# Folding row sums: a small TensorE product, or GpSimd copies a pair ahead and a VectorE addition

## The chip, the cores and the metric

The kernel runs on one core of one Trainium2 chip. The metric is the device time of one execution in microseconds (us). Differences under 1% are read with the 95% interval of several rounds, taken on the same chip as runs of the kernel before. A profile is one execution; the four runs of the kernel before differ by up to 4 us, and the profiled one (1109.11 us) is 1.5 us below their median.

## The reference

Attention with normalised queries and keys (8 batches, 12 heads, 448 positions, head size 64), then a feed-forward block with w_in, softmax-times-input, a layer norm and w_out. The part that the change touches is the first line of the attention:

```python
def rmsnorm(x, g):
    rms = np.sqrt(np.mean(x * x, axis=-1, keepdims=True) + 1e-06)
    return x / rms * g
q_n, k_n = (rmsnorm(q, g_q), rmsnorm(k, g_k))
...
h = x @ w_in            # x: 3584 x 768, w_in: 768 x 1024
...
return (ln @ w_out)     # w_out: 1024 x 768
```

## The kernel before

The kernel goes through 48 pairs of heads. A pair's q and k lie in SBUF with each row of 64 elements split in two halves of 32, on partitions that are 32 apart. So a sum of squares comes out as two partial sums, `part` (128x28), and the two halves have to be added across partitions. A constant matrix and a small product did that:

```python
fold = consts.tile([P, 2, 2, 32], FP32, name="fold")
...
ps_t = ctx.enter_context(tc.tile_pool(name="ps_t", bufs=6, space=bass.MemoryType.PSUM))
...
def row_sums(n):
    d["part"] = small.tile([P, 2 * NB], FP32, tag="part", name="part")
    nc.vector.tensor_reduce(d["part"], d["sq"], AX, OP.add)

def fold_sums(n):
    d["ss"] = ps_t.tile([P, 2 * NB], FP32, tag="t", name="ss")
    nc.tensor.matmul(d["ss"], fold.rearrange("p h x t -> p (h x t)"), d["part"], start=True, stop=True)

def rsqrt_seed(n):
    nc.scalar.activation(d["y"], d["ss"], AF.Ln, scale=1.0 / D, bias=eps)
    nc.vector.tensor_scalar(d["x"], d["ss"], -0.5 / D, -0.5e-6, OP.mult, OP.add)
    nc.scalar.activation(d["y"], d["y"], AF.Exp, scale=-0.5)
# then rsqrt_step (VectorE) and normalise: qkn = qk * y (GpSimd)
```

The `ss` tile is one of six PSUM banks that also serve the scores `s`, the values product `o`, the exponentials' sums `sm`, the transposed activations `pu` and the results `po`. Two other parts matter for the argument: work that GpSimd and VectorE share, and the copies that empty `pu`.

```python
def add(n, kc):                       # sum of the exponentials over four chunks
    if kc == 1:
        nc.gpsimd.tensor_tensor(d["es"], d["E"][:, 0], d["E"][:, 1], OP.add)
    else:
        nc.vector.tensor_tensor(d["es"], d["es"], d["E"][:, kc], OP.add)

def fields():                         # first step of a weight's conversion, VectorE
    nc.vector.tensor_scalar(tmp[:, 1], hi, 0xFFFFF, None, OP.bitwise_and)
    nc.vector.tensor_scalar(e, hi, 20, 0x7FF, OP.logical_shift_right, OP.bitwise_and)
def product():                        # its last step, for w_in on GpSimd
    nc.gpsimd.tensor_tensor(dst[:, c, cols], m, e.bitcast(FP32), OP.mult)

def ff_transpose(t):
    for half in range(2):
        pt = ps_t.tile([P, 4, P], FP32, tag="t", name="pu")
        ...                           # four transposes on TensorE
        (nc.vector.tensor_copy if half else nc.scalar.copy)(d["uT"][:, 4 * half : 4 * half + 4], pt)
```

The main loop issues, per pair n (each `unit` is followed by whatever `later` put off to that unit):

```python
for n in range(N):
    ...
    unit(lambda: scores(n, 0)); qk_transpose(n + 1)
    unit(lambda: scores(n, 1)); fold_sums(n + 2)      # later: seed, step, normalise of n + 2
    ff(0)                                             # feed-forward work of earlier tokens
    unit(lambda: values(n - 1)); row_sums(n + 3)
    unit(lambda: sums(n - 1)); ff(1)
    unit(lambda: scores(n, 2)); unit(lambda: scores(n, 3)); ff(2)
```

## Time and profile before

| | before |
|---|---|
| time, median of 4 runs (range) | 1110.59 us (1107.99 to 1111.8) |
| span of the profiled execution | 1107.3 us |
| the product: passes, busy | 96, 20.7 us |
| to about 160 us | w_in is converted, VectorE bounds, 11.11 us a pair |
| to about 335 us | w_out is converted, mostly VectorE |
| from about 335 to 950 us | TensorE never idle |

The utilisation rows, the stages and one period are shown with the prediction below. Two groups of instructions (line, engine, operation, output and inputs, shapes, count | busy us, mean ns of one | idle time before them, and what ended it). L467 is the `fields` step of w_in, L529 the product:

```profile
L467 DVE TENSOR_SCALAR tmp<-raw 128x512 uint32<-128x512 uint32 x12 | 14.6, 1216 | 0.0
L529 PE MATMUL ss<-part,fold 128*128 128x28 f32 x96 | 20.7, 298 | 13.5 <-DVE part L524 12.1 <-ACT E L576 0.8 <-DVE r L617 0.6
```

The passage from the VectorE stage to the TensorE stage (start, length, engine, line, operation):

```profile
339.51 0.41 PE L529 MATMUL ss<-part,fold 128*128 128x28 f32 x2
339.76 1.07 PE L676 MATMUL pu<-ident,u 128*128 128x128 f32 x8
340.76 3.23 PE L595 MATMUL o<-E,v 112*64 112x448 f32 x16
344.67 5.42 PE L635 MATMUL h<-w_in,xT 128*128 128x512 f32 x12
```

### The profile page before, as it was taken

Reading aid. Unit: us, or ns where it says so; the run is one execution under the profiler, and the core shown is the slowest. Engines: PE = TensorE matmul, PEld = TensorE weight load, DVE = VectorE, ACT = ScalarE, POOL = GpSimd, SP = SyncE. Lnnn points to the kernel's source line nnn. Section 1 sums busy time; section 2 is a strip of 40 time slices with the busy share of each in tenths; the row PEclk is TensorE's granted clock in tenths of the full one; section 3 lists DMA queues with packets and bytes.
Section 4 is the critical chain, followed back from the end, with each engine's and each line's share of the span. In section 5 each row is a group of like instructions: output and inputs, shape, how many; then the busy total and the mean of one; then the engine's idle time right before and its main releaser. Section 6 shows DMA issues by size and latency. Waiting matters only on the chain.

```text
span 1107.3 us, 10659 instructions
## 1 busy us (share of the span) xinstructions
PE 1035.3 (93%) x3617; PEld 475.6 (43%) x3617; DVE 605.4 (55%) x1018; ACT 370.6 (33%) x773; POOL 240.3 (22%) x155
## 2 busy tenths in 40 slices
PE   3988888888789999999999999999999999999997
PEld 1323233333234444444444444444444444455554
DVE  3999996569997444444444444454446644522300
ACT  3656553235564222222222222332224322311110
POOL 2565651123223111111111011121112211100000
PEclk9899999998989999999999999999999999999999
DMA  7454544014543111111111111121111100000010
GB/s 140 89 122 98 124 87 85 23 39 93 112 88 62 40 40 40 39 32 33 32 37 40 40 40 39 40 51 40 40 39 40 34 23 24 14 15 15 15 44 31
DMA packets 230391, 57.49 MB, mean 52 GB/s; under 512 B 223152, under 2 KB 223160, under 8 KB 230328
## 3 DMA queue, kind: packets, MB, share of 16 engines
q1 hardware_dynamic: 225984, 45.64, 20.9%
q10 hardware_dynamic: 4344, 11.08, 2.6%
q8 instruction: 30, 0.49, 0.2%
q14 instruction: 33, 0.27, 0.1%
HBM read 45.68 MB, written 11.01 MB: 51 GB/s over the span
## 4 chain that ended last, share of the span: by engine, by line
PE 75%; DVE 14%; issue 4%; ACT 3%; DMA 1%; SPq 1%; ACTq 0%; DVEq 0%
PE po L686 27%; PE h L635 26%; PE s L572 9%; PE o L595 9%; DVE es L586 2%; PE pu L676 2%; PE sm L604 2%; DVE tmp L467 2%; DVE qkT L559 2%; DVE tmp L475 1%; SPq L505 1%; DVE r L619 1%; DVE tmp L477 1%; DVE r L617 1%; PE ss L529 1%
## 5 line engine op out<-in xcount | busy, mean ns | idle before, releaser
L635 PE MATMUL h<-w_in,xT 128*128 128x512 f32 x672 | 305.0, 604 | 11.7 <-DVE u L653 11.7
L686 PE MATMUL po<-w_out,uT 128*128 128x384 f32 x896 | 298.0, 489 | 2.9 <-ACT uT L677 2.9
L686 PEld LDWEIGHTS po<-w_out,uT 128*128 128x128 f32 x896 | 168.3, 190 | 132.9 <-issue 15.0
L572 PE MATMUL s<-qkT 64*112 64x448 f32 x768 | 204.6, 584 | 16.9 <-ACT E L576 6.7
L576 ACT ACTIVATE E<-s 112x448 f32<-112x448 f32 x384 | 178.0, 550 | 110.0 <-PE s L572 109.9
L635 PEld LDWEIGHTS h<-w_in,xT 128*128 128x128 f32 x672 | 126.2, 193 | 167.5 <-issue 162.8
L584 POOL TENSOR_TENSOR es<-E 112x896 f32<-112x896 f32 x48 | 110.5, 2301 | 325.2 <-ACT E L576 318.7
L595 PE MATMUL o<-E,v 112*64 112x448 f32 x768 | 163.9, 572 | 1.2 <-DVE xT L621 1.2
L572 PEld LDWEIGHTS s<-qkT 64*112 64x112 f32 x768 | 76.6, 177 | 136.9 <-issue 73.6
L677 DVE COPY uT<-pu 128x512 f32<-128x512 f32 x28 | 19.2, 687 | 187.3 <-PE pu L676 187.3
L586 DVE TENSOR_TENSOR es<-es,E 112x896 f32<-112x896 f32 x96 | 115.1, 1199 | 10.9 <-ACT E L576 7.8
L663 POOL TENSOR_TENSOR he<-he,mhalf 128x1 f32<-128x1 f32 x28 | 21.7, 774 | 379.2 <-DVE he L662 379.2
L549 POOL TENSOR_TENSOR qkn<-qk,ny 128x896 f32<-128x896 f32 x48 | 83.0, 1730 | 81.6 <-DVE ny L544 35.0
L648 ACT ACTIVATE u<-h,hmax 128x1024 f32<-128x1024 f32 x28 | 31.2, 1114 | 207.3 <-DVE hmax L645 207.3
L687 ACT COPY y<-po 128x384 f32<-128x384 f32 x56 | 26.8, 479 | 213.5 <-PE po L686 213.5
L595 PEld LDWEIGHTS o<-E,v 112*64 112x64 f32 x768 | 53.2, 143 | 86.5 <-issue 80.5
L645 DVE TENSOR_REDUCE hmax<-h 128x1 f32<-128x1024 f32 x28 | 34.3, 1224 | 84.3 <-PE h L635 84.3
L604 PE MATMUL sm<-es,ones 112*64 112x448 f32 x192 | 44.8, 544 | 16.0 <-DVE es L586 14.1
L617 DVE STREAM_TRANSPOSE r<-sm 128x448 f32<-128x448 f32 x48 | 31.0, 646 | 45.8 <-PE sm L604 45.8
L524 DVE TENSOR_REDUCE part<-sq 128x28 f32<-128x896 f32 x48 | 51.7, 1076 | 5.9 <-ACT sq L519 5.9
L519 ACT ACTIVATE sq<-qk 128x896 f32<-128x896 f32 x48 | 45.8, 955 | 23.1 <-ACT y L687 11.3
L559 DVE STREAM_TRANSPOSE qkT<-qkn 128x896 f32<-128x896 f32 x48 | 52.9, 1102 | 0.0
(54 smaller groups left out, 578.7 us busy)
## 6 DMA issues: line engine op xcount, KB each, us to landing
qk<-in_q_dram SPq DMA_DIRECT2D x192, 56.0 KB, 2.6
qk<-in_k_dram SPq DMA_DIRECT2D x192, 56.0 KB, 2.4
v<-in_v_dram SPq DMA_DIRECT2D x48, 224.0 KB, 3.0
out_dram<-y ACTq DMA_DIRECT2D x28, 384.0 KB, 2.3
raw<-in_moe_w_in_dram SPq DMA_DIRECT2D x12, 512.0 KB, 4.2
raw<-in_moe_w_out_dram SPq DMA_DIRECT2D x16, 384.0 KB, 3.4
grow<-in_g_q_dram ACTq DMA_DIRECT2D x2, 0.2 KB
grow<-in_g_k_dram ACTq DMA_DIRECT2D x2, 0.2 KB
```

The source lines that it names most:

```text
L519: nc.scalar.activation(d["sq"], d["qk"].rearrange("p s b d -> p (s b) d"), AF.Square)
L524: nc.vector.tensor_reduce(d["part"], d["sq"], AX, OP.add)
L549: nc.gpsimd.tensor_tensor(d["qkn"], d["qk"].rearrange("p s b d -> p (s b) d"), d["y"].rearrange("p b -> p b ()").to_broadcast([P, 2 * NB, ...
L559: nc.vector.transpose(d["qkT"].rearrange("p s t -> p (s t)"), d["qkn"].rearrange("p b d -> p (b d)"))
L572: nc.tensor.matmul(s, d["qkT"][hh, 1, kc * SP : (kc + 1) * SP], d["qkT"][hh, 0, :], start=True, stop=True)
L576: nc.scalar.activation(d["E"][:, kc, h], d["s", h], AF.Exp)
L584: nc.gpsimd.tensor_tensor(d["es"], d["E"][:, 0], d["E"][:, 1], OP.add)
L586: nc.vector.tensor_tensor(d["es"], d["es"], d["E"][:, kc], OP.add)
L595: nc.tensor.matmul(d["o"][h * D : (h + 1) * D, :], d["v"][:, h, kc], d["E"][:, kc, h], start=(kc == 0), stop=(kc == NJ - 1),)
L604: nc.tensor.matmul(d["sm"][h * D : (h + 1) * D, :], ones[0:SP, :], d["es"][:, h], start=True, stop=True)
L635: nc.tensor.matmul(d["h"][:, hs], xTs[m][:, c, i * P : (i + 1) * P], w_in[:, c, hs], start=(c == 0), stop=(c == KD - 1))
L686: nc.tensor.matmul(po, d["uT"][:, c], w_out[:, c, hs], start=(c == 0), stop=(c == KF - 1))
```

## The change

Its intent is to take 48 small products off TensorE, the busiest engine. GpSimd copies `part` with its 32-partition groups exchanged, one pair ahead of need, and VectorE adds the two. The result is in SBUF, so no PSUM bank is taken any more.

```diff
-    fold = consts.tile([P, 2, 2, 32], FP32, name="fold")
     ...                                   # and its set-up: a memset and eight copies
+    def swap_sums(n):
+        d = st[n]
+        d["ss"] = small.tile([P, 2 * NB], FP32, tag="ss", name="ss")
+        for g in range(4):
+            o = g ^ 1
+            nc.gpsimd.tensor_copy(d["ss"][g * 32 : g * 32 + 32], d["part"][o * 32 : o * 32 + 32])
     def fold_sums(n):
         d = st[n]
-        d["ss"] = ps_t.tile([P, 2 * NB], FP32, tag="t", name="ss")
-        nc.tensor.matmul(d["ss"], fold.rearrange("p h x t -> p (h x t)"), d["part"], start=True, stop=True)
+        nc.vector.tensor_tensor(d["ss"], d["ss"], d["part"], OP.add)
     def prepare(n):
         squares(n)
         row_sums(n)
+        swap_sums(n)
     ...                                   # pairs 0 and 1: fold_sums outside a unit
                 row_sums(n + 3)
+                later(3, lambda n=n: swap_sums(n + 3))
```

More of the change, by code (lines that the diff above doesn't have):

```diff
@@ L427, in setup @@
         make_identity(nc, ident)
-        nc.gpsimd.memset(fold, 0.0)
-        for g in range(4):
-            gs = slice(g * 32, g * 32 + 32)
-            for x in range(2):
-                nc.gpsimd.tensor_copy(fold[gs, g // 2, x], ident[gs, gs])
         pg = ps_t.tile([P, KF + 2], FP32, tag="t", name="pg")
@@ L777, in fast_path @@
         wtarget = 1
-        unit(lambda: fold_sums(0))
+        fold_sums(0)
         rsqrt_seed(0)
@@ L784, in fast_path @@
         gain(0)
-        unit(lambda: fold_sums(1))
+        fold_sums(1)
+        unit(lambda: None)
         load(3)
```

## The prediction

"Port", in the recorded texts, is my name for what the period in it shows: beside GpSimd's w_in product VectorE's second `es` addition took 1.98 us for 1.08, beside GpSimd's `es` L467 took 1.28 for 0.39, and `es` 2.93 for 2.09. The trace shows the lengths, not what causes them. The +0.5 us for 250 to 335 us, the +0.3 us of the start and the 0.35 us of a rival's copies were assumed; no trace showed them.

> **What bounds the kernel now.** I read the page's busy table first, then busy time by stage, then the waits and the timeline inside the stages.
>
> ```profile
> PE 1035.3 (93%) x3617; PEld 475.6 (43%) x3617; DVE 605.4 (55%) x1018; ACT 370.6 (33%) x773; POOL 240.3 (22%) x155
> PE   3988888888789999999999999999999999999997
> DVE  3999996569997444444444444454446644522300
> ```
>
> TensorE looks like the bound everywhere, but the slices show two kinds of stage: in slices 2 to 6 and 10 to 12 VectorE is full and TensorE is not; from slice 13 on it is the other way round. Busy time by stage (columns: length, then PE, PEld, DVE, ACT, POOL, then clock and DMA) makes that exact:
>
> ```profile
> 45.00:160.00 115.00, 98.41 (x409) 36.29 (x408) 111.50 (x175) 69.81 (x148) 68.78 (x31) 1.00 0.52 108
> 160.00:250.00 90.00, 78.10 (x228) 31.14 (x228) 58.88 (x113) 27.82 (x58) 15.42 (x11) 0.94 0.23 49
> 250.00:335.00 85.00, 70.80 (x256) 25.99 (x255) 79.15 (x140) 47.14 (x102) 25.82 (x13) 0.86 0.48 99
> 335.00:700.00 365.00, 365.00 (x1278) 174.54 (x1275) 169.68 (x283) 105.35 (x219) 57.67 (x40) 1.00 0.17 38
> 700.00:950.00 250.00, 250.00 (x891) 117.78 (x892) 123.73 (x205) 77.55 (x165) 48.51 (x28) 1.00 0.17 38
> ```
>
> From 335 to 950 us TensorE is never idle, and its waits there are empty. From 45 to 160 us VectorE is busy 97% and TensorE waits for it (13.7 us for the addition of the exponentials). 250 to 335 us is VectorE's too (93%). So a TensorE saving counts from 335 us on and a VectorE cost before it, and these must be priced separately.
>
> The product to be removed, in the TensorE stage (start, length, engine, line):
>
> ```profile
> 485.58 1.76 PE L572 MATMUL s<-qkT 64*112 64x448 f32 x8
> 487.27 0.41 PE L529 MATMUL ss<-part,fold 128*128 128x28 f32 x2
> 487.51 1.07 PE L676 MATMUL pu<-ident,u 128*128 128x128 f32 x8
> ```
>
> Its two passes are recorded as 0.41 us, but the next group starts 0.24 us after it: that is its cost. Where w_in's product or the values product follows, the chain of waits gives it 0.34 us (at 209.66 and 243.94 us).
>
> In the VectorE stage every pair takes the same 11.11 us (GpSimd's w_in products start at 54.85, 65.96, 77.08 and so on to 154.85). One period:
>
> ```profile
> 99.30 2.06 POOL L481 TENSOR_TENSOR w_in<-tmp 128x512 f32<-128x512 f32 x1 [2.09 <-DVE tmp L477]
> 101.31 2.93 POOL L584 TENSOR_TENSOR es<-E 112x896 f32<-112x896 f32 x1
> 102.23 1.10 DVE L559 STREAM_TRANSPOSE qkT<-qkn 128x896 f32<-128x896 f32 x1
> 103.25 1.28 DVE L467 TENSOR_SCALAR tmp<-raw 128x512 uint32<-128x512 uint32 x1
> ```
> ```profile
> 100.33 1.98 DVE L586 TENSOR_TENSOR es<-es,E 112x896 f32<-112x896 f32 x1
> ```
>
> VectorE's second es addition takes 1.98 us where the first (99.14) took 1.08, and L467 takes 1.28 where at 47.76, with a lighter neighbour, it took 0.39. Each is long exactly while a GpSimd operation is under way: the es addition ends 0.95 us after w_in ends, L467 ends at 104.53, 0.29 us after GpSimd's es ends at 104.24. In return GpSimd's es takes 2.93 against about 2.09 at 370.39, where nothing disturbs it. The two engines take turns, and about 0.9 + 0.9 us of VectorE's "busy" time per pair is waiting for GpSimd.
>
> [...] the two-input addition and the tensor_scalar stretch, the transpose (1.10 us) doesn't. [...] the eight set-up copies of 32x32 took 1.53 us, 0.19 apart.
>
> **The change, part by part.**
>
> *TensorE loses 48 products* (96 passes). In 335 to 950 us there are 46 passes: 13 products to 700 us, mostly ahead of a transpose, 13 x 0.24 = 3.1 us; 10 after it, ahead of w_in's or the values product, 10 x 0.34 = 3.4 us. All of it is on the path: -6.5 us. The three products in 160 to 250 us stand in a chain that is mostly TensorE's: -1.0 us. Those before 160 us and in 250 to 335 us save nothing, for TensorE waits there.
>
> *VectorE gains 48 additions* of 128x28. Duration 187 ns, and dependent ones of that size start 0.22 us apart (94.97, 95.19). In the VectorE stage 10 periods x 0.22 = +2.2 us; in 250 to 335 us, 7 x 0.22 = +1.5 us. After that hidden.
>
> *GpSimd gains 192 copies* of 32x28, which I price as the 32x32 ones: 4 x 0.19 = 0.77 us per pair, 37 us in all on an engine that is 78% idle. They are placed a pair ahead, so nobody waits for their result. But they are queued on GpSimd right behind w_in and in front of es. When w_in ends (101.36), [...] the four copies run under the transpose, which doesn't contend, and es starts at about 103.1 instead of 102.31, just ahead of L467, which becomes ready at 103.3. L467 is then blocked to the end of es, which comes 0.77 us later. So the copies, though nobody needs them soon, push a GpSimd operation that VectorE has to wait out: 10 periods x 0.77 = +7.7 us. In 250 to 335 us es waits for ScalarE's exponentials (5 to 7 us idle ahead of it), so the copies are done before and only brush VectorE's two-input instructions: +0.5 us.
>
> *A PSUM bank and a wait go.* The sums held one of six rotating banks until VectorE had read them; TensorE waited 4.1 us for that in 250 to 335 us, where it isn't the bound. VectorE's reading no longer waits for ScalarE's logarithm (2.2 us in that stage), but its next step needs ScalarE's result anyway: -1.0 us.
>
> *The start.* For pair 0 copies and an addition replace a product that was waited for, and the copies of pair 2 now stand ahead of the normalising of pair 1 on GpSimd, which must wait for pair 2's data (about 3 us later). VectorE has 3.9 us idle there, and the loads bind, so: +0.3 us.
>
> Sum: -6.5 -1.0 +2.2 +1.5 +7.7 +0.5 -1.0 +0.3 = +3.7 us, hence 1114 us from the 1110.39 of before.
>
> **Rivals.** *The pure saving:* the copies slip in without moving es (say, [...] es, which now runs without VectorE's addition beside it, is shorter). [...] Time: 3.7 - 7.7 = -4.0, 1106 us. *Longer copies:* these shift data by 32 partitions, which the set-up copies don't. At 0.35 us each, es would start after L467 has slipped in, and block the next tensor_scalar instead: about 1.4 us per pair, +14 for +7.7, 1120 us. *A new wait on ScalarE:* the logarithm now waits for VectorE's addition behind L468, not for a product that was done long ago, so ScalarE's queue of exponentials slips by about 0.7 us a period. They have 2 us of slack ahead of GpSimd's es (ready at 110.18, used at 112.42), so I expect no cost; if there is one, it comes on top, 1 us a period, 1124 us. *A full gain of 48 x 0.41 = 20 us,* as the table of groups suggests, would give 1090; I exclude it, as the passes overlap their neighbours and half of them lie where TensorE waits.
>
> **Range and chances.** I give the port mechanism one half (1114), the pure saving a quarter (1106), the longer copies or a new wait a quarter (1120 to 1124). The middle is 1113 us, and the range 1104 to 1122. A gain of 2% needs 1088 us, 15 us below the best rival; a loss of 2% needs 1133, above the worst by 9. So: faster 0.01, same 0.96, slower 0.03.
>
> **What would show it.** TensorE's time from 335 us to the end shorter by 6 to 7 us. In the VectorE stage a period of 12.1 us instead of 11.11, GpSimd's es ending later and L467 some 2.0 us long. If the period stays near 11.3, the port step is wrong and the saving stands alone. If the copies take over 0.27 us each, L467 is short and L468 or the new addition long. If ScalarE's exponentials come just before GpSimd's es, the ScalarE rival holds. The prediction fails if the order of the engines' work in the first 45 us moves the weights' conversion by more than some 3 us, or if a TensorE wait appears after 335 us.

## The result, and the profile after

The changed kernel took 1126.29 us (median of 4 runs, 1124.92 to 1128.36) against 1110.59. The ratio of the means is 1.0146, with a 95% interval of 1.0122 to 1.017. (Ratios here are the mean time of one kernel's runs over that of the other's in the same rounds, so not quite the ratio of the medians quoted.) The class, within 2%, is as predicted. The time is not: 1126 lies outside the range of 1104 to 1122, and above even the worst rival.

Busy shares first, then the stages (columns as in the prediction: length, PE, PEld, DVE, ACT, POOL, then clock and DMA):

```profile
PE 1025.0 (91%) x3521; PEld 462.5 (41%) x3521; DVE 641.4 (57%) x1066; ACT 374.0 (33%) x773; POOL 293.9 (26%) x338
```

```profile
45.00:160.00 115.00, 89.12 (x349) 30.67 (x348) 111.27 (x170) 63.36 (x131) 70.14 (x66) 0.84 0.47 101
335.00:700.00 365.00, 358.43 (x1224) 167.47 (x1220) 188.18 (x309) 107.70 (x224) 73.42 (x96) 0.99 0.19 40
```

TensorE is 10 us less busy and the kernel is 16 us longer. Busy time did leave the bound engine; it was simply not the only thing that counted. In 45 to 160 us VectorE is as full as before, but TensorE gets through fewer matmuls (349 for 409; 22 of the missing 60 are the removed product's passes): everything moves more slowly. Its granted clock over that stretch is 0.84 (1.00 before), but it does not bound that stage.

To find where the time went, I took the start of GpSimd's normalising product for each of the 48 pairs in both traces and subtracted. This lag is a running ledger. "Predicted" is the prediction's own terms, sorted into the same stretches:

| stretch | lag at its end | change, measured | predicted |
|---|---|---|---|
| start, to pair 4 | 3.4 us | +3.4 | +0.3 |
| VectorE stage, pairs 4 to 14 | 15.5 | +12.1 | +9.9 |
| pairs 14 to 25 | 15.5 | 0.0 | 0.0 |
| passage, pair 25 to 26 | 20.8 | +5.3 | nothing |
| TensorE stage, to the end | 15.8 | -5.0 | -6.5 |
| sum | | +15.8 | +3.7 |

The two zeros of pairs 14 to 25 agree by luck. The prediction's is -1.0 + 1.5 + 0.5 - 1.0; the measured one is +1.2 to pair 20, -2.4 at pair 21 and +1.2 to pair 25. The -2.4 comes both with the copies alone (experiment 4, -1.9) and with the product removed alone (experiment 6, -2.6), and was not followed.

**The VectorE stage.** Here is one period of GpSimd and VectorE, as counterpart of the period in the prediction:

```profile
95.10 3.16 DVE L587 TENSOR_TENSOR es<-es,E 112x896 f32<-112x896 f32 x2
95.26 2.05 POOL L474 TENSOR_TENSOR w_in<-tmp 128x512 f32<-128x512 f32 x1 [2.14 <-DVE tmp L470]
97.38 1.68 POOL L526 COPY ss<-part 32x28 f32<-32x28 f32 x4
98.19 1.10 DVE L560 STREAM_TRANSPOSE qkT<-qkn 128x896 f32<-128x896 f32 x1
99.13 2.08 POOL L585 TENSOR_TENSOR es<-E 112x896 f32<-112x896 f32 x1
99.21 2.29 DVE L460 TENSOR_SCALAR tmp<-raw 128x512 uint32<-128x512 uint32 x1
101.76 0.17 DVE L530 TENSOR_TENSOR ss<-ss,part 128x28 f32<-128x28 f32 x1
107.59 2.05 POOL L474 TENSOR_TENSOR w_in<-tmp 128x512 f32<-128x512 f32 x1 [2.14 <-DVE tmp L470]
```

The period is 107.59 - 95.26 = 12.33 us (11.11 before; 12.32 on the mean of nine). The copies stand between w_in's product and `es` and end at 99.06; the first takes 0.94 us, to 98.32, just past the end of VectorE's second `es` addition at 98.26, and the others 0.20 each. Then `es` takes 2.08 us, to 101.21, and VectorE's tensor_scalar, which starts at 99.21, ends 0.29 us after it: it takes 2.29 us, where the same step (then L467) took 1.28. That is the mechanism that the prediction named, with the sign that it named ("L467 some 2.0 us long"). From the end of VectorE's second `es` addition to the end of that tensor_scalar it was 2.22 us before (102.31 to 104.53) and is 3.24 now (98.26 to 101.50): 1.02 us a pair.

The groups say the same for the whole run:

```profile
L460 DVE TENSOR_SCALAR tmp<-raw 128x512 uint32<-128x512 uint32 x12 | 22.6, 1887 | 0.0
L526 POOL COPY ss<-part 32x28 f32<-32x28 f32 x192 | 62.7, 327 | 24.5 <-DVE part L517 15.7
L530 DVE TENSOR_TENSOR ss<-ss,part 128x28 f32<-128x28 f32 x48 | 24.9, 519 | 1.2 <-POOL ss L526 1.1
```

The tensor_scalar went from 1216 to 1887 ns on the mean of 12. A mean of 519 ns for an addition that takes 0.17 us at 101.76 says that it, too, is often stretched; at 357.08 (below) it takes 1.93 us and ends together with a GpSimd `es` that began just before it.

**The passage.** The same place as before, first TensorE, then VectorE just ahead of it:

```profile
355.05 1.09 PE L677 MATMUL pu<-ident,u 128*128 128x128 f32 x8
359.67 4.92 PE L596 MATMUL o<-E,v 112*64 112x448 f32 x16 [3.53 <-DVE uT L678]
```
```profile
356.06 1.10 DVE L560 STREAM_TRANSPOSE qkT<-qkn 128x896 f32<-128x896 f32 x1
357.08 1.93 DVE L530 TENSOR_TENSOR ss<-ss,part 128x28 f32<-128x28 f32 x1
358.94 0.68 DVE L678 COPY uT<-pu 128x512 f32<-128x512 f32 x1
```

TensorE now waits 3.53 us for VectorE's copy of `uT`, and then takes 4.92 us for a product that took 3.23, at a granted clock of 0.65 from 359.67 to 364.59 us, where it had been 1.00 (340.76 to 343.99). Together 3.53 + 1.69 = 5.2 us, the whole of the step in the ledger. There is no data dependence here: `o` does not use `uT`. It needs a bank. In the built program of the kernel before, `o` got the bank of a scores tile, which ScalarE's exponentials had emptied by then (no wait at 340.76); in the changed one it gets the bank of the second half of `pu`, which that very copy empties. Nothing in the source puts it there: with one user fewer, the six banks go round differently.

**The TensorE stage.** In the chain that ended last, two feed-forward products that are one round apart (start, length):

```profile
374.29 5.35 PE h L635 x12
403.84 5.35 PE h L635 x12
```
```profile
394.68 5.35 PE h L636 x12
424.01 5.35 PE h L636 x12
```

Before, they start 29.55 us apart, after, 29.33: each product that is gone saves 0.22 us. Later in the stage it is 0.22 too (756.51 to 786.06 before, 773.89 to 803.22 after).

**TensorE's waits after** (what it waits for: total us, times, longest). The first line was 2.4 us in 2 times before, and 21.8 us of it fall in the first 160 us, where VectorE bounds and a wait of TensorE costs nothing by itself. The second line did not exist before:

```profile
PE s L573 <- DVE r L618: 26.0, 12, 3.4
PE o L596 <- DVE uT L678: 3.5, 1, 3.5
```

### The profile page after: what moved, and what is told of

Same layout as the page of the kernel before. It is cut to its first block, busy times and chain, and to the rows that moved or that the text cites. A ratio compares the mean times of both kernels' runs of the same rounds, so it can differ in the third digit from the quotient of the medians.

```text
span 1123.1 us, 10684 instructions
## 1 busy us (share of the span) xinstructions
PE 1025.0 (91%) x3521; PEld 462.5 (41%) x3521; DVE 641.4 (57%) x1066; ACT 374.0 (33%) x773; POOL 293.9 (26%) x338
## 4 chain that ended last, share of the span: by engine, by line
PE 72%; DVE 17%; issue 5%; ACT 3%; SPq 2%; DMA 1%; ACTq 0%; POOL 0%; DVEq 0%; POOLq 0%
PE po L687 26%; PE h L636 26%; PE s L573 8%; PE o L596 8%; DVE tmp L460 3%; DVE es L587 2%; PE pu L677 2%; DVE qkT L560 2%; PE sm L605 2%; SPq L498 2%; DVE ss L530 1%; DVE r L620 1%; DVE tmp L468 1%; DVE r L618 1%; ACT E L577 1%
## 5 line engine op out<-in xcount | busy, mean ns | idle before, releaser
L573 PE MATMUL s<-qkT 64*112 64x448 f32 x768 | 200.1, 614 | 64.8 <-DVE r L618 26.0
L585 POOL TENSOR_TENSOR es<-E 112x896 f32<-112x896 f32 x48 | 102.8, 2143 | 292.6 <-ACT E L577 278.7
L596 PE MATMUL o<-E,v 112*64 112x448 f32 x768 | 173.7, 599 | 4.2 <-DVE uT L678 3.5
L573 PEld LDWEIGHTS s<-qkT 64*112 64x112 f32 x768 | 74.3, 186 | 178.1 <-ACT E L577 74.9
L596 PEld LDWEIGHTS o<-E,v 112*64 112x64 f32 x768 | 55.7, 151 | 117.9 <-issue 91.4
L649 ACT ACTIVATE u<-h,hmax 128x1024 f32<-128x1024 f32 x28 | 31.2, 1114 | 209.2 <-DVE hmax L646 209.2
L526 POOL COPY ss<-part 32x28 f32<-32x28 f32 x192 | 62.7, 327 | 24.5 <-DVE part L517 15.7
```

The lines of the kernel that those rows point to most:

```text
L526: nc.gpsimd.tensor_copy(d["ss"][g * 32 : g * 32 + 32], d["part"][o * 32 : o * 32 + 32])
L573: nc.tensor.matmul(s, d["qkT"][hh, 1, kc * SP : (kc + 1) * SP], d["qkT"][hh, 0, :], start=True, stop=True)
L596: nc.tensor.matmul(d["o"][h * D : (h + 1) * D, :], d["v"][:, h, kc], d["E"][:, kc, h], start=(kc == 0), stop=(kc == NJ - 1),)
```

## The experiments

Theory: four things add up. *Ports* (the name as in the prediction): the copies push GpSimd's `es` by 1 us a pair while VectorE waits for it. *Bank:* the passage costs 5 us because a bank's user is gone. *Saving:* 0.22 us a product in the TensorE stage. *Start:* a new order of the first pairs costs 3 us. Rivals: the addition on VectorE is what makes the period longer; the passage costs time whatever the banks; ScalarE's logarithm, which now waits for VectorE, slows the stage.

### 1. Copies one unit earlier

```diff
-                later(3, lambda n=n: swap_sums(n + 3))
+                later(2, lambda n=n: swap_sums(n + 3))
```

Now the copies stand behind the normalising product and ahead of w_in's, where GpSimd is otherwise waiting.

> Changed kernel, the four copies placed one unit earlier, so that on GpSimd they stand behind the normalising product and ahead of w_in, no longer between w_in and es. Port-order theory: the period of the VectorE stage falls from 12.32 us to about 11.3 us (11.11 of before plus 0.22 for the addition), 10 periods, so about 10 us off: 1116 us. Rival (the addition itself, or the logarithm waiting behind it on ScalarE, is the cost): the period stays at 12.2 to 12.3 and the time at 1125 us.

Measured: 1113.88 us (1113.79 to 1115.68), ratio to before 1.0038 [1.0013, 1.0063]. The period falls from 12.32 to 11.35 us:

```profile
99.23 1.70 POOL L550 TENSOR_TENSOR qkn<-qk,ny 128x896 f32<-128x896 f32 x1 [2.54 <-DVE ny L545]
100.99 1.40 POOL L526 COPY ss<-part 32x28 f32<-32x28 f32 x4
103.20 1.99 POOL L474 TENSOR_TENSOR w_in<-tmp 128x512 f32<-128x512 f32 x1 [0.81 <-DVE tmp L470]
105.15 2.94 POOL L585 TENSOR_TENSOR es<-E 112x896 f32<-112x896 f32 x1
```

GpSimd has the same copies to do, but they end 0.81 us before w_in's input is there, and `es` follows w_in directly again, at its length of before (2.94; 2.93 in the prediction's period). Same instructions, another place in one queue: 12 us by the medians. What is left of the period's growth, 11.35 - 11.11 = 0.24 us, fits the price of the addition (0.22), but what the copies still cost is in it too. The ledger still jumps by 5.3 us at the passage (4.4 to 9.7), so that is another matter.

### 2. The sums back in a PSUM bank

```diff
+        s = d["ss"]
+        d["ss"] = ps_t.tile([P, 2 * NB], FP32, tag="t", name="sp")
-        nc.vector.tensor_tensor(d["ss"], d["ss"], d["part"], OP.add)
+        nc.vector.tensor_tensor(d["ss"], s, d["part"], OP.add)
```

> Changed kernel, the addition writes its result into a rotating PSUM bank as the product did, so that the banks rotate as before the change. Bank theory: TensorE's waits for the row-sum transposes in the VectorE stage (26 us) and the 3.5 us wait of the values product at 356 us go, and some 4 to 5 us come off at the passage to the TensorE stage: 1121 us. Rival (the banks don't matter, the blocked addition does): 1126 us, and the jump of 5 us between 340 and 370 us stays.

Measured: 1129.41 us (1127.75 to 1129.86), ratio 1.0169 [1.0143, 1.0194]; the expected gain did not come. But the ledger shows the jump gone (24.7 at pair 25, 24.9 at pair 26). The time was lost elsewhere: the period grew to 12.65 us, and the trace has why. With the sums in PSUM, VectorE's next step waits for ScalarE's logarithm, which reads the same tile first (76.4 us over the run; in the change, with the sums in SBUF, it has no such wait):

```profile
104.18 0.19 DVE L540 TENSOR_SCALAR nx<-sp 128x28 f32<-128x28 f32 x1 [0.35 <-ACT ny L539]
```

That is 0.35 us a pair, and the period is 0.33 longer than after. The expected end of TensorE's 26 us of waits in the VectorE stage did not come either: over the whole run 15.2 us of them are left, and 24.2 us of waits for this step are new. A further 2.9 us come at pairs 15 to 16 as w_out's conversion begins, which I did not follow. So the bank theory is right about the passage, and this way of keeping a bank is too dear. A run that only gives one time would have been read as a refutation.

### 3. The first pairs in the order of before

```diff
-        fold_sums(0)
+        unit(lambda: fold_sums(0))
 ...
-        fold_sums(1)
-        unit(lambda: None)
+        unit(lambda: fold_sums(1))
 ...
-        prepare(2)
+        squares(2); row_sums(2)
         wtarget = 2
         normalise(1)
+        swap_sums(2)
```

> Changed kernel with the first pairs ordered as before: the two units around the first folds restored, and the copies of pair 2 behind the normalising of pair 1. Start theory: the 3.4 us by which pair 4 comes later go: 1123 us. Rival (the copies and the addition in the path of the first pairs cost it): less than 1 us off, 1125.5 us.

Measured: 1126.38 us (1123.72 to 1128.0), ratio 1.0143 [1.0113, 1.0172], level with the change. The lag of pair 1 goes from 4.7 to 0.4 us, so the edit did what it should, but the lag at pair 4 is still 2.9. My theory of the start is refuted: making pair 1 some 4 us earlier takes 0.5 us off pair 4 and nothing clear off the time.

### 4. The copies alone, in the kernel before

```diff
                 row_sums(n + 3)
+                later(3, lambda n=n: swap_sums(n + 3))   # into a tile that nobody reads
```

> Kernel of before, product kept, with the four GpSimd copies added in the place that the change gives them, their result unused. Port-order theory: the period of the VectorE stage goes from 11.11 to about 12.1 us without any VectorE addition, 10 us more: 1120 us. Rival (copies are harmless, the addition is the cost): 1111 us.

Measured: 1122.51 us (1120.82 to 1124.92), ratio 1.0111 [1.0082, 1.014]. The product is still there, and nobody uses the copies. The period is 12.11 us, +1.00; the ledger goes from 3.1 at pair 4 to 13.1 at pair 14, and stays at 14.1 through the whole TensorE stage:

```profile
94.34 2.05 POOL L481 TENSOR_TENSOR w_in<-tmp 128x512 f32<-128x512 f32 x1 [2.14 <-DVE tmp L477]
96.46 1.68 POOL L531 COPY sw<-part 32x28 f32<-32x28 f32 x4
98.21 2.07 POOL L591 TENSOR_TENSOR es<-E 112x896 f32<-112x896 f32 x1
98.29 2.28 DVE L467 TENSOR_SCALAR tmp<-raw 128x512 uint32<-128x512 uint32 x1
```

The pattern is that of the change, line for line, without any part of its data flow. This rules the addition and ScalarE's logarithm out as the main cost of the period. The passage costs 0.8 us here: the bank is still in use.

### 5. The addition alone, in the kernel before

```diff
                 fold_sums(n + 2)
+                extra(n + 2)      # VectorE: sw = part + part, 128x28, nobody reads it
```

> Kernel of before, product kept, with an unused VectorE addition of two SBUF operands of 128x28 per pair at the place of the new one. If the addition costs its issue only: the period of the VectorE stage goes from 11.11 to 11.33 us, 2.2 to 4 us in all: 1113 us. Rival (it is often blocked behind GpSimd's es and costs up to 1.9 us each time): 1118 us or more.

Measured: 1114.2 us (1113.28 to 1115.03), ratio 1.0029 [1.0012, 1.0046]. The period grows by 0.10 us only, less than the 0.24 that experiment 1 left, where others wait for the addition. No step at the passage (5.1 to 5.2). It is a small term.

### 6. The product removed, and nothing put in its place

```diff
-        d["ss"] = ps_t.tile([P, 2 * NB], FP32, tag="t", name="ss")
-        nc.tensor.matmul(d["ss"], fold.rearrange("p h x t -> p (h x t)"), d["part"], start=True, stop=True)
+        d["ss"] = d["part"]
```

The result is wrong (relative error 1.79): this is the ceiling of what any replacement could gain.

> Kernel of before with the product left out and nothing in its place, the unfolded sums used (a wrong result, on purpose). Pure saving: 0.22 us per product in the TensorE stage, 22 products, 5 us: 1105.5 us. Bank theory: the jump of about 5 us at the passage to the TensorE stage comes from the lost bank in the rotation and not from the copies or the addition, so that it shows here too and eats the saving: 1110.5 us. If the jump needs the blocked addition, it is about 3 us or nothing here.

Measured: 1108.97 us (1108.3 to 1111.53), ratio 0.9992 [0.9973, 1.0012]: no gain that can be told from none. The ledger: 1.7 us at pair 4 and at pair 14 (the period is 11.11, the products there cost nothing), then down to -0.8 at pair 25, up to +3.6 at pair 26, and down by 0.2 a pair to -0.4 at pair 47. The step is there without copies and without an addition:

```profile
338.94 1.09 PE L675 MATMUL pu<-ident,u 128*128 128x128 f32 x8
342.43 4.92 PE L594 MATMUL o<-E,v 112*64 112x448 f32 x16 [2.40 <-DVE uT L676]
```

2.40 us of wait and 4.92 - 3.23 = 1.69 of slow run are 4.1 of the 4.4 us of the step. So the removal itself costs 4.4 us once and saves about 4 in the TensorE stage; it also gains 2.6 at pair 21, which stays unexplained (see the ledger above). In the change the wait is 1.1 us longer, as the blocked addition (1.93 us) stands ahead of the copy.

### 7. Copies earlier, addition on GpSimd

As experiment 1, and the addition moves from VectorE to GpSimd, directly behind the copies:

```diff
             nc.gpsimd.tensor_copy(d["ss"][g * 32 : g * 32 + 32], d["part"][o * 32 : o * 32 + 32])
+        nc.gpsimd.tensor_tensor(d["ss"], d["ss"], d["part"], OP.add)
     def fold_sums(n):
-        nc.vector.tensor_tensor(d["ss"], d["ss"], d["part"], OP.add)
+        pass
```

> The changed kernel with the copies placed early, as in the first experiment, and the addition moved to GpSimd behind the copies, so that VectorE has nothing new. Period of the VectorE stage back at 11.1 to 11.2 us (2.4 us off the first experiment), no blocked addition at the passage (up to 2 us off), the TensorE saving of 5 us kept: 1108 us, a little better than before. If GpSimd's longer work behind the normalising product blocks VectorE's joins instead: 11.4 us and 1112 us.

Measured: 1109.09 us (1108.3 to 1110.57), ratio 0.9988 [0.9971, 1.0006], correct. The period is 0.12 us above before; the jump at the passage is 3.9 us (1.0 to 4.9), with a wait of 2.69 us for the copy of `uT`. Of the change's larger costs only the passage is left.

### 8. The same, with the logarithm written to a PSUM bank

```diff
+        lg = ps_t.tile([P, 2 * NB], FP32, tag="t", name="lg")
-        nc.scalar.activation(d["y"], d["ss"], AF.Ln, scale=1.0 / D, bias=eps)
+        nc.scalar.activation(lg, d["ss"], AF.Ln, scale=1.0 / D, bias=eps)
 ...
-        nc.scalar.activation(d["y"], d["y"], AF.Exp, scale=-0.5)
+        nc.scalar.activation(d["y"], lg, AF.Exp, scale=-0.5)
```

This gives the banks their sixth user back without an instruction more; only ScalarE touches it, and VectorE's next step, which waited 76.4 us for the logarithm in experiment 2, waits 1.8 us here, for GpSimd's sums.

> The version of e7 (copies one unit earlier, addition on GpSimd) with ScalarE's logarithm writing its result into a tile of the six rotating PSUM banks, and its exponential reading it there: no instruction more, but the rotation of the banks is again the one of the kernel before. Bank theory: the passage into the TensorE stage costs nothing any more (the lag jumps by under 1 us at pair 25 to 26 instead of the 3.9 of e7, and the values product there doesn't wait for VectorE's uT copy), the saving of about 5 us afterwards stays, so about 1105 us, ratio about 0.995. Rival (the jump is a matter of when the stage begins, not of the banks): the jump stays, 1109 us, as e7.

Measured: 1106.74 us (5 runs, 1106.1 to 1107.38), ratio 0.9968 [0.9954, 0.9982], correct. The passage:

```profile
343.02 1.09 PE L679 MATMUL pu<-ident,u 128*128 128x128 f32 x8
344.04 3.23 PE L598 MATMUL o<-E,v 112*64 112x448 f32 x16
```

No wait, 3.23 us, and the ledger moves by 0.5 (2.9 to 3.4) where it moved by 3.9. In the built program `o` again gets the bank of a scores tile. The saving afterwards stays: from 3.4 at pair 26 to -0.5 at pair 47. My expectation said "again the one of the kernel before"; in the built program it isn't quite that, as the place of the logarithm in the order is another, but what mattered was that `o` should not get the bank of `pu`. The time is 1.7 us above the 1105 that I expected, of which 1.5 us come at pair 15 to 16, as in experiment 2. This version beats both kernels, by 0.3% and, by the medians, 1.7%.

### 9. Experiment 7 with the two copies of the transposed activations exchanged

```diff
-            (nc.vector.tensor_copy if half else nc.scalar.copy)(d["uT"][:, 4 * half : 4 * half + 4], pt)
+            (nc.scalar.copy if half else nc.vector.tensor_copy)(d["uT"][:, 4 * half : 4 * half + 4], pt)
```

> The version of e7 with the two copies of the transposed u exchanged: VectorE takes the first half, ScalarE the second. Bank theory: the values product at the passage takes the bank of the second half, which ScalarE now frees; if ScalarE is sooner, the jump at pair 25 to 26 falls from 3.9 to about 1 us, so 1106 us; ScalarE's copy stands behind exponentials though, and then the jump stays about 3 to 4 us and the time 1109. Rival (not the bank): the jump stays at 3.9 whatever the engine, with no wait for a copy of either engine.

Measured: 1106.95 us (5 runs, 1106.12 to 1109.09), ratio 0.9972 [0.9957, 0.9986]. Neither text fits. The jump is 3.9 us as in experiment 7, and `o` still waits 2.65 us for VectorE's copy of `uT`. In the built program `o` now gets the bank of the *first* half of `pu`, which VectorE empties in this version. I had taken the bank for fixed and changed the engine; the bank went with the engine. So this run doesn't test what it should. A gain over experiment 7 is not shown: the intervals of the two ratios overlap, and the profiled execution is the slowest of the five (1109.09 us), with a span of 1107.2 us for experiment 7's 1107.1. In it 1.6 us more are lost up to pair 47 (lag 2.6 for 1.0), and they come back after the last pair; experiment 10 gains 1.6 there too.

### 10. The kernel before with the same exchange

> The kernel before with the same exchange of the copying engines, as the control of e9. Bank theory: the values product at the passage doesn't take that bank in the kernel before, so nothing of note changes: 1110 to 1112 us, ratio 0.999 to 1.002. If the exchange helps or harms by itself (VectorE's or ScalarE's queue), it shows here: more than 3 us either way.

Measured: 1114.25 us (5 runs, 1113.31 to 1115.28), ratio 1.004 [1.0026, 1.0055]: slower by 0.4%, 4 us, which is more than the expected nothing and than the 3 us from which I called it an effect. One new wait of 1.8 us of the transposes for VectorE's `uT` copy appears, and the ledger shows 1.9 us at pair 25 to 26. So the exchange is no gain by itself. As a control this run gave something else: its instructions on every engine stand in the order of the kernel before (only the halves that two copies take are exchanged, long after the start), yet its ledger reads 1.5 us from pair 2 on. So about 1.5 us of every lag at the start is how single executions fall. The profiled execution of before was itself 1.5 us below its median.

## Why the prediction was wrong

It got the direction, the class and the main mechanism right, and was 12 us too low (1114 for 1126). By its own steps:

- **"TensorE loses 48 products: -6.5 us."** Right in kind, a little too large: -5.0. The term that was mis-sized is 0.34 us for the ten products ahead of w_in's or the values product. The chain gives 0.22 for those too: what follows a removed product got longer (the `h` group from 5.24 to 5.35 us in the later rounds), so 0.34 counted 0.11 that came back. The timeline of before could have shown it: seven of the ten stand ahead of w_in's product, which starts 0.24 us after them.
- **"VectorE gains 48 additions: +2.2 and +1.5 us."** Right in size where it was tested: between the 0.10 us a period of experiment 5 and the 0.24 of experiment 1. The +1.5 was not tested by itself; that the ledger has nothing in that stretch is a sum of other things (see there).
- **"The copies push a GpSimd operation that VectorE has to wait out: +7.7 us."** Right mechanism, shown by experiments 1 (taken away: -0.96 a period) and 4 (alone: +1.00 a period). So the pure saving, in which `es` isn't moved, falls. The mis-sized term is the 0.77 us by which `es` was to end later; it is 1.02. `es` starts 0.87 us after VectorE's addition has ended (98.26 to 99.13), 0.10 more than priced. And `es`, which used to start beside VectorE's addition (101.31, the addition ending at 102.31), now needs its whole 2.08 us, where 1.93 were left of it before: 0.15. So 10 periods cost about 10 us for 7.7.
- **"Longer copies": 1120 us.** This rival expected `es` to fall behind the tensor_scalar at copies of 0.35 us, which was assumed. It did not, though by only 0.08 us (99.13 to 99.21): the copies across partitions are recorded with 0.20 us each, 0.24 apart, and only the first one of a period is longer (0.94 us), as it waits for the addition. The order stayed.
- **"A new wait on ScalarE."** The logarithm does wait for VectorE (38.6 us in all), and it costs nothing that the ledger shows: the copies alone make nearly the whole period. The rival falls.
- **"The start: +0.3 us."** The ledger has 3.4 at pair 4. The reason I gave (the order of the first pairs) costs nothing, by experiment 3. About 1.5 us is that one profile of before, by experiment 10, and most of the other 1.9 arises at pairs 2 to 4, where experiment 4 with its copies alone has 1.6. So I read it as the cost of the moved `es`, which begins a period or two before the pairs that I counted; that reading is argued, not tested, and can hold for a part at most: experiment 1, whose copies stand elsewhere, still has 2.8 at pair 4. The rest stays open.
- **"A PSUM bank and a wait go: -1.0 us."** This is the step that failed. I took a bank set free for a gain in slack, priced its wait where TensorE did not bind, and never asked who else would get which bank. In its place the runs showed a cost of 5.3 us at the passage, 4.4 of it from the removal alone (experiment 6), gone when a bank has a user in the same place (experiments 2 and 8). The built programs of all twelve kernels agree. In six (the change, experiments 1, 3, 6, 7 and 9) this one `o`, of pair 22 and no other, takes over a bank from `pu`; in their traces it waits 2.40 to 3.53 us and takes 4.92. In the other six it takes over the bank of a scores tile, does not wait and takes 3.23. That the slow run follows from the wait is what these traces agree on; it was not tested by itself. The prediction's closing sentence, that it fails "if a TensorE wait appears after 335 us", names exactly what happened, but nothing in its sum or its rivals stood for it.

One small sum of its chances is off too: 1088 us is 18 us below the 1106 of its best rival, not 15. Nothing rests on it.

Measured minus predicted, in the order of the ledger: 3.1 + 2.2 + 0.0 + 5.3 + 1.5 = 12.1 us, the 15.8 of the trace less the 3.7 of the sum.

What stays open: the 1.3 to 2.9 us that several variants (2, 3, 4, 5, 8, 10) lose as w_out's conversion begins, the 2.4 us that others gain at pair 21, and which event decides that `o` gets the bank of `pu`: I read the banks from the built programs, not the reason for the choice.

## What to carry to other kernels

Before you give a small, cheap instruction to an idle engine, look at what stands behind it in that engine's queue and who waits for that: 0.9 us of copies cost 1 us a period behind one instruction and at most 0.24 ahead of it. Removing an instruction also removes its buffer from a shared pool, and all later users may get other buffers, with other waits (here 2.40 us for one `o`, experiment 6); compare the waits of the built program, not only the instructions. And when several effects overlap, a running difference of one marker per iteration between two traces shows where each part of the time went, where a single total misleads (experiment 2).

## What the traces show of small instructions beside large ones

- VectorE's tensor_scalar took 2.29 us beside GpSimd's `es` (99.21 in the change), and 0.39 at 47.76 in the kernel before, where `es` began only at 48.09. The small addition took 1.93 us beside `es` (357.08) and 0.17 at 101.76. VectorE's transpose took 1.10 us with `es` beside it (102.23 in the kernel before) as with GpSimd idle (15.85), and 1.09 to 1.11 in all 48 times. For queues this means that a small operation of GpSimd's that isn't itself in anyone's way can move a large one into the way (four copies of together 0.92 us: +1.00 us a period alone, 0.24 with the addition when placed otherwise).
- Four copies of 32x28 f32 that shift partitions took 0.92 us beside a VectorE transpose (718.27 in the change), and 1.68 where VectorE's `es` addition ran beside the first (97.38). The median of one is 0.20 us, as for the set-up copies of 32x32 without a shift; those start 0.19 apart on average, these 0.24. That the shift costs the difference is not shown.
- Fewer users of a pool of PSUM banks can make its waits longer: without the 48 small tiles one group waited 2.40 us (3.53 in the change) for a bank that it had not needed before.
